# Norm operations one score step sooner, and the last double value phase respaced, in a fused attention and gated-MLP kernel

## Chip, cores, metric

The kernel runs on one core of one Trainium2 chip. The metric is device time in microseconds (us). Before: 265.57 us (three runs, 265.5 to 265.64).

## The reference

```python
xn = layernorm(x)                          # x: (1, 2048, 512) bf16, no affine part
q, k, v = split(xn @ wqkv)                 # 32 heads of 16
scores = q @ k.T * 16 ** -0.5              # causal, window of 256 keys
o = softmax(scores) @ v
h = (xn @ w_gate) * (xn @ w_up)            # F = 1792
return x + o @ wo + h @ w_down
```

## The kernel before

It works in four chunks of 512 rows. TensorE's stream is laid out by hand: 75 *score steps* (a batch of 24 or 16 small matmuls into one PSUM tile `S`, then one exponential on ScalarE into a tile `P`), and between them "fillers": QKV, gate, up and down projections, in groups of two or four matmuls of 512 columns. At some steps the softmax-times-V products follow. Where two groups of four heads come due together there are 192 of these small matmuls in a row; I call that a *double value phase*. There are five in the kernel, near 90, 124, 155, 187 and 222 us.

Steps are numbered `g`; `SHIFT[g]` gives more or less filler after step `g`, and `GAP` is a least amount of it. `self.beside[g]` holds small work that is put into the streams at the end of step `g`; the layer norms of the next chunk go there.

```python
GAP = 9.6
SHIFT = {20: -2, ..., 62: 3, 63: 6, 64: 8, 66: 8, 67: 6, 68: 4, 69: 2}      # cut

self.ps_m = pool("ps_m", 4, space=PSUM)      # four banks for all results but S

def norm_scale(self, t, n=4):                # rs = (var + eps) ** -0.5, on GpSimd
    ...
    (nc.gpsimd if t else nc.vector).tensor_scalar(out=ve, in0=mv[:, :, 1], scalar1=1e-5, op0=add)
    nc.gpsimd.tensor_tensor(out=rs, in0=ve, in1=self.mhalf[:, 0:n], op=pow)

def norm_apply(self, t):                     # xn = (x - mean) * rs, on VectorE
    nc.vector.tensor_scalar(out=xn, in0=self.x[:, t, :], scalar1=mean, scalar2=rs, ...)

def scores(self, T, pieces):
    ...                                      # matmuls into S
    nc.scalar.activation(out=P[:, :, 0:col], in_=S[:, :, 0:col], func=Exp, scale=0.25)
    for at in self.places(pieces, 4):        # masks of the far edge, on GpSimd
        for half in ...: self.triangle(P[half, :, at:at + 64], False)

def values(self, T, c, accs=None):           # one group of four heads
    accs = [self.ps_m.tile(...) for _ in range(2)]          # two of the four banks
    ...                                      # 96 matmuls; then two transposes on VectorE

def store(self, T, b, part=0):               # evacuates a bank: x += psd, then DMA out
    nc.vector.tensor_tensor(out=y, in0=ps, in1=y, op=add)

# in fillers(): norms of chunk T + 1, b = 0..3
#   statistics and rs of tile b at step i = b, normalise and DMA transpose at i = b + 1
for i, fs in norms(T + 1, 0, 1).items():
    self.beside[self.first[T, 0] + (5, 6, 7, 8, 9)[i]] = fs

# in run(), for each step g
upto = max(total * (g + 1) / len(steps) + SHIFT.get(g, 0), spent + GAP)
...
for _, f in self.beside.get(g, ()): f()
fill(upto, g)
```

A double value phase takes all four banks of `ps_m`, so it cannot run ahead of the evacuation of the last four results (near 90 us TensorE waits 0.21 us for one, as shown below).

The softmax here doesn't subtract the row's maximum and nothing guards it: scores larger than these inputs give would overflow.

## Time and profile before

| | before |
|---|---|
| time, median | 265.57 us |
| span in the profile | 263.7 us, clock 1.00 |
| TensorE busy | 259.6 us (98%) |
| share of the chain of waits on TensorE | 97% |
| first score batch starts / last matmul starts | 13.53 / 260.84 us |

TensorE bounds it. Its busy time says little more: in this trace the 128x512 matmul lasts 380 ns while the starts of two in a row are 216 ns apart, so that the busy times of two overlap. What counts is whether a start comes late. From 10 us on they hardly ever do, except inside three of the double value phases.

In the lines of the profile, PE is TensorE with its matmuls and PEld its weight loads, DVE is VectorE, ACT is ScalarE and POOL is GpSimd; L366 is line 366 of the kernel. Here are the double value phases in the chain of work that ended last (start us, length us, what, number of instructions):

```profile
89.78 2.56 PE acc L366 x190
124.48 2.40 PE acc L366 x175
155.57 2.60 PE acc L366 x162
187.72 2.40 PE acc L366 x175
221.40 2.57 PE acc L366 x177
```

Two are 2.40 us and three are longer, by 0.16, 0.20 and 0.17 us, in all 0.53. The same matmuls are in each. (Where a phase is cut into pieces this view shows only a piece; the phase lengths in the tables below are taken from the first value matmul to the first start after the last, which gives 2.557, 2.399, 2.600, 2.399 and 2.568.)

VectorE ahead of and in the first two long phases, from its timeline (start us, length us, engine, line, operation, output<-inputs, shapes, count, and in brackets the idle time just before and what ended it):

```profile
86.97 0.48 DVE L190 TENSOR_SCALAR xn<-x,mv,rs 128x512 bf16<-128x512 bf16 x1 [1.27 <-POOL rs L182]
...
88.19 0.39 DVE L343 TENSOR_TENSOR P<-P,diag 128x512 bf16<-128x512 bf16 x1
89.85 0.48 DVE L190 TENSOR_SCALAR xn<-x,mv,rs 128x512 bf16<-128x512 bf16 x1 [1.27 <-POOL rs L182]
90.25 0.67 DVE L444 TENSOR_TENSOR x<-psd,x 128x512 bf16<-128x512 f32 x1
...
154.07 0.41 DVE L190 TENSOR_SCALAR xn<-x,mv,rs 128x512 bf16<-128x512 bf16 x1 [1.27 <-POOL rs L182]
154.39 0.69 DVE L444 TENSOR_TENSOR x<-psd,x 128x512 bf16<-128x512 f32 x1
154.99 0.68 DVE L232 CAST gsb<-gp 128x512 bf16<-128x512 f32 x1
```

GpSimd ahead of the first, from its timeline (four masks, then the two operations that make rs):

```profile
86.90 1.95 POOL L158 TENSOR_SCALAR_AFFINE_SELECT P<-P 64x256 bf16<-64x256 bf16 x4
88.94 0.22 POOL L179 TENSOR_SCALAR ve<-mv 128x1 f32<-128x1 f32 x1
89.25 0.57 POOL L182 TENSOR_TENSOR rs<-ve,mhalf 128x1 f32<-128x1 f32 x1
```

The statistics were done at 88.27; the masks kept GpSimd until 88.85, and rs was ready at 89.82, when the normalise could start. VectorE ran nothing from 88.58 to 89.85, though the result that its next operation, the store-add, reads was finished by TensorE at 88.56: it kept the built order. TensorE's weight loads at the three late places, from their timeline:

```profile
90.98 0.10 PEld L366 LDWEIGHTS <-V 64*32 64x32 bf16 x4 [0.21 <-DVE x L444]
...
155.50 0.10 PEld L366 LDWEIGHTS <-V 64*32 64x32 bf16 x4 [0.20 <-issue]
155.73 0.10 PEld L366 LDWEIGHTS <-VS 64*32 64x32 bf16 x4
...
222.68 0.11 PEld L366 LDWEIGHTS <-VS 64*32 64x32 bf16 x3
222.94 0.09 PEld L366 LDWEIGHTS <-VS 64*32 64x32 bf16 x1 [0.15 <-issue]
```

The first names its cause: the store-add (L444, which adds a finished result to x and so frees its bank) that ends at 90.92. The second names none, but its second start comes 0.06 us after a gate copy (L232, which takes a gate result out of its bank) has ended (154.99 + 0.68 = 155.67). The third: three loads of a group of four, a pause, then the fourth, and the profile finds nothing that it waited for.

### The profile page before, as it was taken

What the parts mean: (1) busy time and instruction counts of PE and PEld (TensorE: products, weight loads), DVE (VectorE), ACT (ScalarE), POOL (GpSimd) and SP (SyncE); (2) the same over time, 40 slices, a digit from 0 to 9 for tenths busy, and PEclk for the clock granted to TensorE, in tenths of its full rate; (3) what the DMA queues carried; (4) which work ended last, traced back from release to release, by engine and by line L of the source; (5) the groups of instructions that cost most, each with busy time, mean ns of one, the idle gap of its engine ahead of it and who ended that gap; (6) DMA issues with size and microseconds to landing.
All of it is one profiled execution on the core that took longest, in us unless ns stands there. A gap on an engine that the chain in (4) does not pass through costs nothing.

```text
span 263.7 us, 8896 instructions
## 1 busy us (share of the span) xinstructions
PE 259.6 (98%) x3890; PEld 120.3 (46%) x3890; DVE 174.2 (66%) x341; ACT 175.9 (67%) x142; POOL 117.3 (44%) x278
## 2 busy tenths in 40 slices
PE   7999999999999999999999999999999999999995
PEld 7444444444444544444544454444544445444453
DVE  6677888777726697557963679766685235887244
ACT  3467688888757776677775567767777546887500
POOL 6225343325447744333455654544453452554600
PEclk9999999999999999999999999999999999999999
DMA  6999911220002710002000320001100100000002
GB/s 206 374 354 341 268 21 22 24 47 4 0 22 54 69 24 0 4 0 47 5 0 22 81 65 2 0 2 24 27 4 0 42 21 25 2 0 2 4 2 80
DMA packets 19431, 15.12 MB, mean 57 GB/s; under 512 B 7360, under 2 KB 19392, under 8 KB 19392
## 3 DMA queue, kind: packets, MB, share of 16 engines
q1 hardware_dynamic: 18848, 14.26, 20.3%
q8 instruction: 30, 0.49, 0.8%
q10 hardware_dynamic: 544, 0.30, 0.4%
q14 instruction: 9, 0.07, 0.1%
HBM read 9.70 MB, written 2.10 MB: 45 GB/s over the span
## 4 chain that ended last, share of the span: by engine, by line
PE 97%; DVE 1%; DMA 1%; issue 0%
PE gp L395 19%; PE up L406 19%; PE psd L428 17%; PE qkp L251 11%; PE S L312 10%; PE acc L366 7%; PE vp L239 5%; PE psd L434 5%; PE L L428 2%; DMA x<-in_A_x_dram 1%; DVE st L169 1%; PE L L434 1%; PE L L366 0%; PE xTp L209 0%; DVE xn L190 0%; DVE mv L170 0%
## 5 line engine op out<-in xcount | busy, mean ns | idle before, releaser
L319 ACT ACTIVATE P<-S 128x2048 bf16<-128x2048 f32 x75 | 140.7, 1876 | 51.5 <-PE S L312 44.6
L158 POOL TENSOR_SCALAR_AFFINE_SELECT P<-P 64x256 bf16<-64x256 bf16 x224 | 101.3, 452 | 126.0 <-ACT P L319 111.6
L395 PE MATMUL gp<-xnT,Wg 128*128 128x512 bf16 x224 | 60.2, 380 | 0.0
L406 PE MATMUL up<-xnT,Wu 128*128 128x512 bf16 x224 | 58.8, 380 | 0.0
L411 DVE TENSOR_TENSOR hT<-up,gsb 128x512 bf16<-128x512 f32 x56 | 38.3, 684 | 18.6 <-PE up L406 11.6
L428 PE MATMUL psd<-Wd,hT 128*128 128x512 bf16 (+1 forms) x210 | 48.0, 369 | 0.0
L343 DVE TENSOR_TENSOR P<-P,diag 128x512 bf16<-128x512 bf16 (+1 forms) x75 | 29.1, 388 | 9.5 <-ACT P L319 9.5
L428 PEld LDWEIGHTS <-hT 128*128 128x128 bf16 x238 | 21.3, 98 | 25.1 <-issue 2.9
L406 PEld LDWEIGHTS <-Wu 128*128 128x128 bf16 x224 | 20.6, 98 | 25.6 <-issue 2.3
L395 PEld LDWEIGHTS <-Wg 128*128 128x128 bf16 x224 | 20.1, 98 | 24.9 <-issue 2.1
L312 PE MATMUL S<-Q,K 16*64 16x320 bf16 (+4 forms) x720 | 31.0, 260 | 0.0
L312 PE MATMUL S<-Q,Ko 32*64 32x320 bf16 (+4 forms) x720 | 31.0, 260 | 0.0
L251 PE MATMUL qkp<-xnT,Wqkv 128*128 128x512 bf16 x128 | 29.9, 380 | 0.0
L230 ACT ACTIVATE gsb<-gp 128x512 bf16<-128x512 f32 x40 | 23.5, 596 | 7.5 <-PE gp L395 6.7
L312 PEld LDWEIGHTS <-K 16*64 16x64 bf16 x720 | 12.1, 103 | 30.7 <-issue 30.7
L372 DVE STREAM_TRANSPOSE at<-acc 128x512 f32<-128x512 f32 x30 | 19.3, 690 | 6.8 <-PE acc L366 6.8
L444 DVE TENSOR_TENSOR x<-psd,x 128x512 bf16<-128x512 f32 (+1 forms) x15 | 9.7, 653 | 16.4 <-PE psd L434 16.4
L251 PEld LDWEIGHTS <-Wqkv 128*128 128x128 bf16 x128 | 11.7, 98 | 14.5 <-issue 1.6
L366 PE MATMUL acc<-P,V 64*32 64x320 bf16 (+4 forms) x672 | 18.0, 253 | 0.0
L366 PE MATMUL acc<-P,VS 64*32 64x320 bf16 (+4 forms) x672 | 18.0, 253 | 0.0
L366 PEld LDWEIGHTS <-V 64*32 64x32 bf16 x720 | 15.0, 91 | 2.4 <-issue 2.0
L239 PE MATMUL vp<-Wqkv,xnT 128*128 128x512 bf16 x64 | 15.3, 380 | 0.0
(54 smaller groups left out, 198.2 us busy)
## 6 DMA issues: line engine op xcount, KB each, us to landing
out_dram<-x SPq DMA_DIRECT2D x15, 128.0 KB, 1.7
Wg<-in_B_w_gate_dram SPq DMA_DIRECT2D x2, 896.0 KB, 10.9
Wu<-in_B_w_up_dram SPq DMA_DIRECT2D x2, 896.0 KB, 12.5
Wd<-in_B_w_down_dram SPq DMA_DIRECT2D x1, 1792.0 KB, 17.6
Wqkv<-in_A_wqkv_dram SPq DMA_DIRECT2D x3, 512.0 KB, 5.4
x<-in_A_x_dram SPq DMA_DIRECT2D x2, 512.0 KB, 8.3
VS<-V SPq DMA_DIRECT2D x6, 144.0 KB, 2.6
x<-in_A_x_dram SPq DMA_DIRECT2D x3, 256.0 KB, 7.1
```

The lines of the kernel that those rows point to most:

```text
L158: nc.gpsimd.affine_select(out=v, in_=v, pattern=pattern + [[1 if diag else -1, 64]], compare_op=ALU.is_ge if diag else ALU.is_gt, fill=0.0 ...
L230: nc.scalar.activation(out=out, in_=in_, func=ACT.Copy)
L239: nc.tensor.matmul(ps[:], lhsT=self.xnT[T][:, b, k, :], rhs=self.Wqkv[:, k, 1024:1536], start=(k == 0), stop=(k == 3))
L251: nc.tensor.matmul(ps[:], lhsT=self.Wqkv[:, k, lo:lo + 128], rhs=self.xnT[T][:, :, k, :], start=(k == 0), stop=(k == 3))
L312: nc.tensor.matmul(S[64 * par:64 * par + 64, e, col:col + n], lhsT=(self.Ko if par else self.K)[U, c][rows, keys], rhs=self.Q[T, c][rows, ...
L319: nc.scalar.activation(out=P[:, :, 0:col], in_=S[:, :, 0:col], func=ACT.Exp, scale=0.25)
L343: self.nc.vector.tensor_tensor(out=v, in0=v, op=ALU.min, in1=self.diag.unsqueeze(1).unsqueeze(1).to_broadcast([128, 4, n, 64]))
L366: nc.tensor.matmul(accs[par][32 * e:32 * e + 32, q:q + n], lhsT=v, rhs=P[rows, e, col:col + n], start=(i == 0), stop=(i == len(todo) - 1), ...
L395: nc.tensor.matmul(ps[:], lhsT=self.Wg[:, k, 128 * f:128 * f + 128], rhs=self.xnT[T][:, :, k, :], start=(k == 0), stop=(k == 3))
L406: nc.tensor.matmul(ps[:], lhsT=self.Wu[:, k, 128 * f:128 * f + 128], rhs=self.xnT[T][:, :, k, :], start=(k == 0), stop=(k == 3))
L411: nc.vector.tensor_tensor(out=self.hT[T, f][:], in0=ps[:], in1=self.gsb[:], op=ALU.mult)
L428: nc.tensor.matmul(ps, lhsT=self.hT[T, f][:, 128 * b:128 * b + 128], rhs=self.Wd[:, f, c0:c1], start=(f == 0), stop=False)
```

## The change

Its intent: take the norms out of the steps just ahead of a double value phase, put one more group of fillers ahead of the phase near 222 us, and keep score batches further apart.

```diff
-GAP = 9.6
+GAP = 10.6
-SHIFT = {..., 62: 3, 63: 6, 64: 8, 66: 8, 67: 6, 68: 4, 69: 2}
+SHIFT = {..., 62: 3, 63: 6, 64: 12, 66: 12, 67: 11, 68: 9, 69: 6, 70: 3}
@@ in fillers()
-                        self.beside[self.first[T, 0] + (5, 6, 7, 8, 9)[i]] = fs
+                        self.beside[self.first[T, 0] + (4, 5, 6, 7, 8)[i]] = fs
```

More of the change, by code (lines that the diff above doesn't have):

```diff
@@ L25 @@
 FIRST = 3
-GAP = 9.6
+GAP = 10.6
 PAIRS = ((0,), (1,), (2,), (3,)), ((0, 1), (2, 3)), ((0, 1), (2, 3)), ((0, 1), (2,))
-SHIFT = {20: -2, 21: -5, 22: -8, 23: -11, 24: -14, 26: -10, 27: -7, 28: -3, 62: 3, 63: 6, 64: 8, 66: 8, 67: 6, 68: 4, 69: 2}
+SHIFT = {20: -2, 21: -5, 22: -8, 23: -11, 24: -14, 26: -10, 27: -7, 28: -3, 62: 3, 63: 6, 64: 12, 66: 12, 67: 11, 68: 9, 69: 6, 70: 3}
 MASKED, FIRST_DIVIDE, SECOND_DIVIDE = 8, 8, 24
```

## The prediction

> **What bounds it now.** TensorE. The page shows PE busy 259.6 of 263.7 us, PE 97% of the chain of waits, clock 1.00. PE busy time alone proves little: [...]here a 128x512 matmul lasts 380 ns (groups view) while starts in the PE timeline are 216 ns apart. So I read starts: after 10 us, PE almost never waits. The visible waits sit in the double value phases (192 value matmuls for two heads groups). In the chain of waits the undisturbed ones take 2.40 us (at 124.5 and 187.7 us); three take longer: 2.56 (89.8), 2.60 (155.6) and 2.57 (221.4). Excess: 0.16 + 0.20 + 0.17 = 0.53 us. That is about all that reordering can win; the rest of the span is matmul work, the start (about 6 us of loads and norms) and the last 2.6 us.
>
> **What the change does.** It adds and removes nothing costly. PE's order is identical up to 220 us; then one group of four gate/up matmuls is placed before the value phase and the score batches after it are respaced, with the same 3890 matmuls and the same kinds of transitions. From about 243 us the order is again the same. Two gate copies go from ACT (596 ns) to DVE (687 ns), both off PE's path. GAP and SHIFT act only in this stretch. Norm operations of chunks 2 and 3 move one score step (about 2.6 to 3.5 us) earlier on DVE, POOL and the DMA queue.
>
> **On the critical path, by mechanism.**
> 1. Norms. DVE works in order, and the normalising operation waits for POOL's rs, queued behind triangle masks (452 ns each): 11.4 us in total, 2.7 at most (waits view). In before, the last of these stands just ahead of the value phase. At 89.85 it holds the store-add (90.25 to 90.92), whose PSUM bank the second heads group needs; PE resumes at 90.98. At 154.07 it holds store-add and gate copy (154.99 to 155.67); PE resumes at 155.73. With the last norm a step sooner, both evacuations can run 1 us or more earlier. Expected gain: 0.14 + 0.2, about 0.35 us.
> 2. Value phase at 221.4. Its excess falls inside groups of four matmuls, at 222.8 to 223.2, where the profile names only "issue". P is ready by then (masks end at 220.0 and 221.2). I expect the shift to help little: 0 to 0.17 us, estimate 0.05.
> 3. Respaced scores, 226 to 242 us: exp (1.88 us) already fits in the 2.62 us spacing without a PE wait, so a wider one wins nothing. More copies on DVE add up to 1.4 us in a stretch where it is 80 to 90% busy; slack looks like about 1 us. Risk of a new wait of 0.1 to 0.4 us.
>
> **Prediction.** 265.57 - 0.35 - 0.05, with 0.05 back for risk: 265.2 us, range 264.8 to 265.7. Faster by over 2%: 0.01; within 2%: 0.985; slower: 0.005.
>
> **What the profile should show.** Value phases near 90 and 155 us at 2.40 to 2.45 us; the DVE wait for rs about 3 us earlier, with store-add and gate copy finished before the second group starts; the phase near 222 us 0.86 us later, still 2.40 to 2.57; PE busy about 259.2; no PE start gap over 0.31 us after 10 us; the end from 243 us unchanged in shape.
>
> **What would make it wrong.** The excess at 90 or 155 us staying: then the bank was not held by the norms. A new wait at 226 to 242 us on the gate/up evacuations. An earlier DVE wait for rs delaying masks or stores at 76 to 87 or 139 to 152 us. The excess near 222 us vanishing wholly (then 265.0).

## The result, and the profile after

The changed kernel took 265.22 us (five runs, 264.85 to 265.39), against 265.5 for before in the same rounds (five runs). The ratio is 0.9989, with a 95% interval of 0.9976 to 1.0003. By time alone this first measurement does not tell the two kernels apart, and the profile even shows the same span, 263.7 us.

The chain of waits of the changed kernel, the same five phases:

```profile
90.28 2.40 PE acc L366 x175
124.83 2.40 PE acc L366 x175
155.91 2.40 PE acc L366 x175
187.87 2.40 PE acc L366 x175
222.41 2.40 PE acc L366 x175
```

All three excesses are gone, the third too. VectorE at the places that answer to those shown of before:

```profile
87.48 0.48 DVE L190 TENSOR_SCALAR xn<-x,mv,rs 128x512 bf16<-128x512 bf16 x1 [1.27 <-POOL rs L182]
87.89 0.41 DVE L343 TENSOR_TENSOR P<-P,diag 128x512 bf16<-128x512 bf16 x1
89.10 0.69 DVE L444 TENSOR_TENSOR x<-psd,x 128x512 bf16<-128x512 f32 x1 [0.80 <-PE psd L434]
...
151.48 0.54 DVE L190 TENSOR_SCALAR xn<-x,mv,rs 128x512 bf16<-128x512 bf16 x1 [2.22 <-POOL rs L182]
...
152.55 0.69 DVE L444 TENSOR_TENSOR x<-psd,x 128x512 bf16<-128x512 f32 x1 [0.20 <-PE psd L434]
153.87 0.69 DVE L232 CAST gsb<-gp 128x512 bf16<-128x512 f32 x1 [0.63 <-PE gp L395]
```

The last normalise is the one at 87.48 and at 151.48. The evacuations after it now wait for TensorE's own result and no longer for GpSimd. The store-add ends at 89.79, 0.42 us before its phase begins (90.21); in before it ended 1.22 us after the begin (90.92 against 89.70). The gate copy ends at 154.56, 1.28 us before its phase (155.84), instead of 0.17 us after the begin. VectorE has not been relieved of its waits. They have been moved; in the waits view, before first and then after:

```profile
DVE xn L190 <- POOL rs L182: 11.4, 6, 2.7
```

```profile
DVE xn L190 <- POOL rs L182: 10.9, 6, 2.7
```

Where is the 0.53 us in this trace? At the start. TensorE's first projection, from the PE timelines of before and then of after:

```profile
6.75 1.02 PE L239 MATMUL vp<-Wqkv,xnT 128*128 128x512 bf16 x4
```

```profile
7.26 1.02 PE L239 MATMUL vp<-Wqkv,xnT 128*128 128x512 bf16 x4 [0.51 <-DMA Wqkv<-in_A_wqkv_dram]
```

Here the run of the changed kernel waited 0.51 us for a weight load. Neither program differs from the other there. So I compare TensorE's *own time*, from the first score batch to the last matmul: 260.84 - 13.53 = 247.31 us before, and 260.82 - 14.03 = 246.78 us after (to the nanosecond, 0.53 less). That is the sum of the three excesses, and no new wait has appeared.

### The profile page after: what moved, and what is told of

Its sections match the earlier page's. It is cut to its first block, busy times and chain, and to the rows that moved or that the text cites. A ratio compares the mean times of both kernels' runs of the same rounds, so it can differ in the third digit from the quotient of the medians.

```text
span 263.7 us, 8896 instructions
## 1 busy us (share of the span) xinstructions
PE 259.4 (98%) x3890; PEld 120.9 (46%) x3890; DVE 175.1 (66%) x342; ACT 175.5 (67%) x141; POOL 116.9 (44%) x278
## 4 chain that ended last, share of the span: by engine, by line
PE 96%; DMA 2%; SPq 0%; issue 0%; DVE 0%
PE gp L395 19%; PE up L406 19%; PE psd L428 17%; PE qkp L251 11%; PE S L312 10%; PE acc L366 6%; PE vp L239 5%; PE psd L434 5%; PE L L428 2%; DMA Wqkv<-in_A_wqkv_dram 2%; PE L L434 1%; PE L L366 0%; SPq L74 0%; PE xTp L209 0%; DVE x L444 0%
## 5 line engine op out<-in xcount | busy, mean ns | idle before, releaser
L230 ACT ACTIVATE gsb<-gp 128x512 bf16<-128x512 f32 x39 | 22.9, 596 | 8.2 <-PE gp L395 7.4
```

The lines of the kernel that those rows point to most:

```text
L230: nc.scalar.activation(out=out, in_=in_, func=ACT.Copy)
```

## Experiments

The questions: which part of the change cleared which phase; whether it is the wait for rs or the work of the norms; what the third excess is, as prediction and profile had only "issue" for it; and whether the late start is chance. Nine kernels ran. All gave correct results. The four kernels of the first group ran on one chip with nine runs of before between them (median 265.2 us); the last two likewise (265.37 us).

| run | median us | ratio to before, 95% | first score batch | own time | phases near 90, 155, 187, 222 us |
|---|---|---|---|---|---|
| before (first profile) | 265.57 | | 13.53 | 247.31 | 2.557, 2.600, 2.399, 2.568 |
| after (first profile) | 265.22 | 0.9989 (0.9976 to 1.0003) | 14.03 | 246.78 | 2.400, 2.398, 2.400, 2.398 |
| gap_only | 265.47 | 1.0010 (0.9997 to 1.0022) | 13.54 | 247.35 | 2.558, 2.790, 2.397, 2.428 |
| norms_only | 264.83 | 0.9990 (0.9976 to 1.0004) | 13.34 | 246.79 | 2.399, 2.398, 2.400, 2.400 |
| shift_only | 265.16 | 1.0004 (0.9990 to 1.0018) | 13.42 | 247.14 | 2.557, 2.597, 2.398, 2.399 |
| scale_sooner | 264.93 | 0.9990 (0.9977 to 1.0002) | 13.46 | 246.89 | 2.400, 2.398, 2.400, 2.505 |
| before_44 | one run | | 13.45 | 247.37 | 2.555, 2.600, 2.399, 2.401 |
| before_36 | one run | | 13.83 | 247.96 | 2.559, 2.790, 3.038, 2.398 |
| after_36 | one run | | 13.69 | 247.64 | 2.400, 2.398, 3.251, 2.400 |
| after_again | 264.77 | 0.9978 (0.9964 to 0.9991) | 13.41 | 246.77 | 2.398, 2.396, 2.398, 2.398 |
| after_wv_act | 267.79 | 1.0087 (1.0073 to 1.0101) | 16.43 | 246.77 | 2.399, 2.395, 2.397, 2.399 |

Phase lengths and own time are sums of starts read from each trace. The phase near 124 us was 2.397 to 2.400 in every run. In after_wv_act the phases come about 3 us later, and its time is of four runs.

### gap_only

```diff
-GAP = 9.6
+GAP = 10.6
```

> Only the constant GAP goes from 9.6 to 10.6. The built instruction order of every engine is the same as before's, so this is also a control: same time as before within the spread of runs (ratio 1.000, at most 0.0015 either way), and in the profile value phases of 2.56, 2.60 and 2.57 us again near 90, 155 and 222 us. If one of these three is 2.40 us here, that excess is a matter of the single run and not of the order.

The built order of every engine is the same as before's, so the part "score batches kept further apart" of the change does nothing by itself; with the new SHIFT it changes nothing either. As a control it shows the noise: a ratio of 1.0010 for the same program. It also holds two warnings. The phase near 222 us was 2.428 here and not 2.568, so that excess depends on the run. And the one near 155 us was 2.790. This time the profile's timeline names its cause, again the gate copy, which VectorE ran 0.2 us later:

```profile
154.27 0.41 DVE L190 TENSOR_SCALAR xn<-x,mv,rs 128x512 bf16<-128x512 bf16 x1 [1.75 <-POOL rs L182]
154.60 0.68 DVE L444 TENSOR_TENSOR x<-psd,x 128x512 bf16<-128x512 f32 x1
155.20 0.68 DVE L232 CAST gsb<-gp 128x512 bf16<-128x512 f32 x1
```

```profile
155.93 0.10 PEld L366 LDWEIGHTS <-VS 64*32 64x32 bf16 x4 [0.33 <-DVE gsb L232]
```

### norms_only

```diff
-                        self.beside[self.first[T, 0] + (5, 6, 7, 8, 9)[i]] = fs
+                        self.beside[self.first[T, 0] + (4, 5, 6, 7, 8)[i]] = fs
```

> Only the norm operations go one score step sooner; SHIFT and GAP are before's. Theory (the last normalise waits on DVE for POOL's rs and so holds back the PSUM evacuations that the value phase needs): the phases near 90 and 155 us fall to 2.40 us, the one near 221 us stays at 2.57; PE's own time, from the first score batch to the last matmul, falls by 0.36 us. Rival (the three excesses have one common cause, such as the fetch of instructions, which the whole change happens to move): the phases near 90 and 155 us stay above 2.5 us, because PE's order is untouched. Ratio to before about 0.9987.

The phases near 90 and 155 us fell to 2.399 and 2.398 us with TensorE's order untouched, as the theory said, and the rival is out. The phase near 222 us was 2.400 here, not the expected 2.57, so own time fell by 0.53 us and not by the expected 0.36: in this run the norms alone look as good as the whole change. Nothing in its surroundings differs from before's, so this is a second hint that its excess is a matter of the run.

### shift_only

```diff
-SHIFT = {..., 64: 8, 66: 8, 67: 6, 68: 4, 69: 2}
+SHIFT = {..., 64: 12, 66: 12, 67: 11, 68: 9, 69: 6, 70: 3}
```

> Only SHIFT is the new one (with it GAP changes no order, as the built order shows). Theory: the phases near 90 and 155 us stay at 2.56 and 2.60 us, the one near 222 us falls to 2.40; PE's own time from the first score batch to the last matmul falls by 0.17 us. Rival (the norms are what cleared all three, by whatever they do to DVE and POOL): the phase near 222 us stays at 2.57. Ratio to before about 0.9994, not to be told from 1 by time alone.

As expected in the trace: 2.557 and 2.597 stay, the last phase is 2.399, and own time falls by 0.17 us. Since norms_only has it at 2.400 without the shift, this run alone does not prove that the shift did it. The time (ratio 1.0004) shows nothing: 0.17 us is less than the spread of the start.

### scale_sooner

This keeps each normalise at the step it has in before, and asks for statistics and rs one step sooner, so that rs passes GpSimd's masks in time.

```diff
-def norms(T, at, step):
+def norms(T, at, step, late=1):
-        out.setdefault(at + step * b + (0, 0, 1, 1)[k], []).append((0, f))
+        out.setdefault(at + step * b + (0, 0, late, late)[k], []).append((0, f))
-for i, fs in norms(T + 1, 0, 1).items():
-    self.beside[self.first[T, 0] + (5, 6, 7, 8, 9)[i]] = fs
+for i, fs in norms(T + 1, 0, 1, 2).items():
+    self.beside[self.first[T, 0] + (4, 5, 6, 7, 8, 9)[i]] = fs
```

> From before: statistics and POOL's rs of a tile are asked for one step sooner, but each normalise stays at the step it has in before, so the wait for POOL goes and DVE's work just ahead of the value phase stays. Theory (the wait for rs is what held the evacuations): the wait of 1.27 us ahead of the last normalise is gone, and the phases near 90 and 155 us are 2.40 to 2.45 us. Rival (it is the work placed there, the 0.41 us normalise itself and its neighbours, that crowds DVE): they stay at 2.5 us or more. The phase near 221 us stays 2.57.

The wait is gone while the normalise stays just ahead of the phase. VectorE's timeline in this run, and the rs that it needed:

```profile
86.51 0.42 DVE L343 TENSOR_TENSOR P<-P,diag 128x512 bf16<-128x512 bf16 x1 [1.35 <-ACT P L319]
86.96 0.48 DVE L190 TENSOR_SCALAR xn<-x,mv,rs 128x512 bf16<-128x512 bf16 x1
88.52 0.69 DVE L444 TENSOR_TENSOR x<-psd,x 128x512 bf16<-128x512 f32 x1 [1.08 <-PE psd L434]
```

```profile
86.35 0.57 POOL L182 TENSOR_TENSOR rs<-ve,mhalf 128x1 f32<-128x1 f32 x1
```

Both phases are 2.400 and 2.398. So it was the wait for rs, passed on through VectorE's order to the evacuation of a bank, and not the normalise itself. The statistics of the last tile (0.68 + 0.18 us) did move a step away in this version, so the work nearby is not quite the same; but in before VectorE stood idle for 1.27 us ahead of that normalise, so it was not short of time there. The phase near 222 us was 2.505, not the expected 2.57.

### before_44, before_36, after_36

These three test the third excess, which by now I took for late instruction fetch. Each trace has 30 packets of 16,384 bytes on an instruction queue (q8 on the page), for the 7,779 to 7,795 instructions of TensorE that it lists, about 260 to a packet. I take each packet for the fetch of one block of TensorE's instructions, and a block for 256 of them: an estimate, from that ratio and from the places in the table below, which lie 1,792 and 1,024 apart, both multiples of 256. A value phase uses its instructions faster than anything else in this kernel: 384 matmuls and weight loads in 2.40 us, against 48 in 0.36 us in a batch of 24 score matmuls and two in 0.216 us in the projections. Four more or fewer idle matmuls at the very start (each a matmul and a weight load) move all later instructions by eight places within the blocks and leave the order of everything else as it is.

```diff
-self.keep_busy(40)
+self.keep_busy(44)      # before_44; 36 in before_36 and in after_36 (on the changed kernel)
```

> before with 44 instead of 40 idle matmuls at the very start, [...]so that the instruction fetch ahead of the value phase near 222 us starts about 0.86 us (four matmuls of 0.216) sooner against that phase. Theory (the excess there is TensorE waiting for its own instructions: a fetch that ends at or after the start of the phase): the fetch ends some 0.6 us or more before the phase starts and the phase takes 2.40 us, as in the changed kernel. Rival (data or a PSUM bank comes late there): it stays between 2.43 and 2.57 us, as data and banks are the same. The phases near 90 and 155 us stay above 2.5 us either way.

> before with 36 instead of 40 idle matmuls at the start: every later TensorE instruction stands eight places earlier in its block, so the fetch ahead of the phase near 222 us starts about 0.86 us later against it. Theory (late instruction fetch): the fetch ends about 1 us after the phase has started and the phase gets much longer, 3.0 us or more (2.57 plus about 0.86 at most). Rival (data or a bank): 2.43 to 2.57 us as before.

> The changed kernel with 36 instead of 40 idle matmuls, so its fetch comes about 0.86 us later against the phase near 222 us, about where before has it. Theory (late instruction fetch): the excess comes back, 0.05 to 0.2 us, so 2.45 to 2.60 us. Rival (data or a bank, which the shift gave time): stays 2.40 us. The phases near 90 and 155 us stay 2.40.

before_44 did as expected near 222 us: 2.401 us, the fetch having ended 0.57 us before the phase. Yet its own time did not fall (247.37 us), because a new pause of 0.21 us (two starts 0.43 us apart, not 0.22) stands near 128.8 us, outside the value phases, inside a group of four gate matmuls. Its weight load:

```profile
128.81 0.10 PEld L395 LDWEIGHTS <-Wg 128*128 128x128 bf16 x1 [0.54 <-issue]
```

The two others missed the place. The phase near 222 us stayed at 2.40 in both, and the phase near 187 us, which had been 2.40 in every other run, took 3.04 and 3.25 us. There the data, the banks and the order of every engine are the same as in the kernels that they came from. The weight loads in after_36:

```profile
188.81 0.11 PEld L366 LDWEIGHTS <-VS 64*32 64x32 bf16 x3
189.75 0.09 PEld L366 LDWEIGHTS <-VS 64*32 64x32 bf16 x1 [0.84 <-issue]
```

It is the same picture as near 222 us in before: three of four, then a pause. What settles it is a count. Counting from 0 all TensorE instructions that the trace lists (matmuls, weight loads and, before these places, three that synchronise) in the order of their starts, and taking the packets of the instruction queue from the trace:

| run, near us | late instruction stands at place | fetch, us | resumes at, us | after the fetch's end |
|---|---|---|---|---|
| before, 222 | 6593 = 25 x 256 + 193 | 220.59 to 221.54 | 222.94 | 1.40 |
| gap_only, 222 | 6593 | 220.42 to 221.60 | 223.00 | 1.40 |
| scale_sooner, 222 | 6593 | 219.80 to 220.97 | 222.45 | 1.48 |
| before_44, 128.8 | 3777 = 14 x 256 + 193 | 126.19 to 127.38 | 128.81 | 1.43 |
| before_36, 187 | 5569 = 21 x 256 + 193 | 187.87 to 189.02 | 190.22 | 1.20 |
| after_36, 187 | 5569 | 187.12 to 188.30 | 189.75 | 1.45 |
| after, 222 (no wait) | 6593 | 220.50 to 221.93 | 223.72 | 1.79 |
| before_44, 222 (no wait) | 6593 | 219.58 to 220.90 | 222.85 | 1.94 |
| norms_only, 222 (no wait) | 6593 | 219.54 to 220.83 | 222.20 | 1.37 |

The late instruction always stands at 193 modulo 256; I take that place for the first of a fetched block; why it is 193 and not 0 was not shown. It starts 1.2 to 1.5 us after the last packet of that block's fetch. If each of the first 29 fetches belongs to the block in its turn, as in the table, then in all eleven traces no such place is passed sooner than 1.20 us after its fetch. The places that TensorE reached 1.79 and 1.94 us after show no pause; norms_only reached it at 1.37 and just made it. In the four traces of the unedited start with before's order near 222 us the place is passed 1.37 to 1.48 us after the fetch, and in the three of the same start with the new SHIFT (after, shift_only, after_again) 1.79 to 2.03 us after, so the shift does take the phase out of danger.

The late loads near 90 and 155 us are of another kind: in before they stand at 203 and 243 modulo 256, and in before_44 each stands eight places further on, as its place in the program does, while the places of the pauses for blocks stay at 193. The rival, data or a bank, would have to strike at one and the same place modulo 256 near 128.8, 187 and 222 us, and to move to another stretch when four idle matmuls are added or taken away at 1 us. In before the last bank that the phase near 222 us can have waited for was free at 221.68 us, when a gate copy on ScalarE ended, 1.26 us before TensorE resumed. That rival is out.

What stays open is why the late fetch moved to the phase near 187 us. I had expected every fetch to move by four matmuls (0.86 us); in fact that one moved from 185.4 to 187.1 and 187.9 us. No run here shows what sets the moment at which a fetch starts.

### after_again

The changed kernel, unedited.

> The changed kernel once more, unedited. The start, where it is the same program as before, differs by run: the first score batch has begun between 13.3 and 14.0 us in the profiles so far, and at 14.03 in the first profile of this kernel, which hid its gain. If that is chance, this profile has it between 13.3 and 13.6 us, TensorE's own time from there to the last matmul is 246.8 us again with all five double value phases at 2.40, and the span is about 263.1. If the change itself delays the start, it is at about 14.0 again. Time 265.0 us, ratio to before 0.998 to 0.999.

All as expected: first score batch at 13.41 us, own time 246.77, span 263.1, and 264.77 us against 265.37, a ratio of 0.9978 with an interval that leaves out 1. The late start of the first profile was chance. Over the seven profiles of kernels with an unedited start, the first score batch begins between 13.34 and 14.03 us, a spread of 0.7 us, more than the whole gain of the change.

### after_wv_act

As the start had the largest spread left, I tried to load the V third of the QKV weights first, from another queue.

```diff
+nc.scalar.dma_start(out=self.Wqkv[:, :, 1024:1536], in_=wq[:, :, 1024:1536])
 for lo, hi in ((0, 1), (1, 2), (2, 4)):
     nc.sync.dma_start(out=self.x[:, lo:hi, :], in_=xv[:, lo:hi, :])
-for lo in (1024, 512, 0):
+for lo in (512, 0):
```

> The changed kernel with the third of the QKV weights that the first projection reads issued first, from ScalarE's DMA queue, ahead of the other loads, instead of fourth on SyncE's. In the profile of the changed kernel TensorE's first projection waited 0.5 us for it. Theory (the spread of the start comes from that load): first projection at 6.5 to 6.65 us, first score batch at 13.3 to 13.45 us, value phases as in the changed kernel, span about 263.0 us, time about 264.8, ratio to before about 0.9975 and a smaller spread of its five runs. If the load only takes bandwidth from the x tiles that the norms wait for, the start comes later than 13.5 us instead.

The last sentence came true, and by more than I thought. The first statistics wait for x, from VectorE's timeline:

```profile
3.31 0.69 DVE L170 BATCH_NORM_STATS2 st<-x 128x6 f32<-128x512 bf16 x1 [1.47 <-DMA x<-in_A_x_dram]
...
5.83 0.69 DVE L170 BATCH_NORM_STATS2 st<-x 128x6 f32<-128x512 bf16 x1 [1.42 <-DMA x<-in_A_x_dram]
```

The second tile's statistics began at 5.83 instead of 3.91 us. The packets of the half megabyte of weights ran from 2.2 to 5.0 us, among those of the first 128 KB tiles of x, which are on the path (two of these tiles landed a median 3.5 us after their issue instead of 2.1 in after_again); the first score batch came at 16.43 us and the kernel took 267.79 us. From there on it is the changed kernel (own time 246.77). No version that I ran beats the changed kernel beyond the noise.

## Why the prediction was right

It said 265.2 us in 264.8 to 265.7, within 2%. Measured were 265.22 and, in the second set of rounds, 264.77 us, just below the range. That the first lies so near the estimate is in part luck: the own time fell by half as much again as predicted (point 4), and a late start (by 0.51 us in the profiled run) hid part of it.

1. **Norms: right in mechanism and size.** It expected about 0.35 us from the phases near 90 and 155 us, by way of VectorE's wait for rs and the evacuation behind it. norms_only gives (2.557 - 2.399) + (2.600 - 2.398) = 0.36 us; scale_sooner shows that the wait is the cause. The signs named in advance are there: phases at 2.40, evacuations 1.4 to 1.6 us sooner against the phase.
2. **Value phase near 222 us: right on what it was not, wrong on size.** It said that P was ready, and that is so. It then expected the shift to "help little: 0 to 0.17 us, estimate 0.05". Measured: 2.568 - 2.398 = 0.17 us between the two first profiles. The missing link was that "issue" here is, by the count above, an instruction block that was fetched late (in before TensorE resumed 1.40 us after its last packet), and that 0.86 us more matmuls ahead of the phase are more time for its fetch: the phase began 0.74 us after the start of the fetch in before, 1.84 us after it in after, and 1.43 us in shift_only. The prediction had listed "the excess near 222 us vanishing wholly" among the things that would make it wrong, and it did vanish. The excess also varies by run with no change at all (0 to 0.17 us in the four kernels with before's order there), so part of the gain is the removal of a chance.
3. **Respaced scores: right that it wins nothing; the risk did not come.** No new wait shows between 226 and 242 us, and own time falls by the whole 0.53 us. The 0.05 us put back for it was too careful. The prediction also gave GAP a share in that stretch; it has none, as the built order does not change with it. And it counted two gate copies moving to VectorE; in the traces it is one (ScalarE 40 to 39, VectorE 16 to 17).
4. **The sum.** Predicted 0.35 + 0.05 - 0.05 = 0.35 us; own time fell by 0.53. The medians fell by 0.28 and 0.60 us in the two sets of rounds, because the start of a run adds or takes some tenths. The prediction left that spread out of its mechanism and had it only in the range.

## What to carry to other kernels

VectorE worked in order here and passed a wait on (its 1.27 us for rs held the evacuations behind it): look for a small operation that waits for a slow engine's queue just ahead of an evacuation that the busy engine needs, and ask for its input one step sooner. Where TensorE had to execute 384 short instructions in 2.40 us, its own instruction fetch became, by the count above, the limit, for up to 0.84 us (after_36); a pause inside a group of equal instructions, with no releaser, at a fixed place modulo 256, was the sign, and four matmuls of 0.216 us more ahead of the burst removed it near 222 us. Moving the code within its blocks is no safe cure: in before_44 the pause near 222 us went and one near 128.8 us came. And when the expected gain is smaller than the spread of the start, compare traces from a common point after the start; the times of a few runs will not show it.
